# A Nyström attention and MLP kernel: stores issued later, block diagonals by per-head copies, a first batch loaded and cast in finer parts

## Chip, cores, metric

One Trainium2 chip, one core. The metric is the device time of the kernel in microseconds (us), median of several runs. The granted TensorE clock is given where it matters.

## The reference

Eight batches of eight heads (sequence 576, head size 64). Attention is the Nyström form with 32 landmarks, followed by a normalised MLP with a residual:

```python
q_lm, k_lm = q, k averaged over 32 segments of 18 rows
A  = softmax(q k_lm^T / 8);  Bm = softmax(q_lm k_lm^T / 8);  C = softmax(q_lm k^T / 8)
Z  = Bm^T / (norm1(Bm) * norminf(Bm) + 1e-6)
for _ in range(6):
    Z = 2 * Z - Z @ Bm @ Z
x   = A @ Z @ C @ v                      # heads side by side: (8, 576, 512)
out = x + relu(layernorm(x) * g @ w_ch1) @ w_ch2      # 512 -> 2048 -> 512
```

## The kernel before

The MLP of all blocks is one stream of matmuls on TensorE (PE): `fill(n)` issues the next n pieces of it. The attention of later batches is cut into steps, and between two steps the kernel calls `fill`, so PE computes MLP while VectorE (DVE) prepares what attention needs next. GpSimd (POOL) casts the loads of q, k and v to fp16 and sums them. W is the number of units of four heads handled at once: 2, or 4 where two batches go together.

A Newton step of the inverse works on 32x32 blocks, one per head, four heads stacked on the 128 partitions. To do four heads in one matmul, the blocks are spread to a block-diagonal 128x128 matrix, `ebd`. This is done by a product with a 0/1 mask over a broadcast source:

```python
def diagonal(name, src, W, mask):
    t = asm.tile([P, W, 4, LM], FP16, name=name, tag=name, bufs=1)
    dve.tensor_tensor(out=t[:], in0=src[:, :, None, :].broadcast_to([P, W, 4, LM]),
                      in1=mask, op=ALU.mult)
    return t
...
for it in range(6):                                   # in attention2, cut
    lo = 0 if it < 5 else LM
    psn = p1([P, W, LM + D], "psn")
    for w in range(W):
        MM(psn[:, w, lo:], ebd[:, w, :, :].rearrange("p a l -> p (a l)"), st[:, w, lo:])
    stn = asm.tile([P, W, LM + D], FP16, name="st", tag="st")
    dve.scalar_tensor_tensor(out=stn[:, :, lo:], in0=st[:, :, lo:], scalar=2.0,
                             in1=psn[:, :, lo:], op0=ALU.mult, op1=ALU.subtract)
    st = stn
    if it < 5:
        ebd = diagonal("ebd", st[:, :, 0:LM], W, masks(W))
    else:
        bmbd = diagonal("bmbd", bm16, W, maskw[:, 0:W, :, None].broadcast_to([P, W, 4, LM]))
    ...
    yield                                             # the caller fills with MLP here
```

So each step is a chain: psn on PE, st on DVE, ebd on DVE, the next psn on PE. The MLP's output block `ot` is stored (`store(j, ot)`) as soon as it is computed, from SyncE's queue, which also issues the loads and the transposes `xnT` by DMA. In the profiles, psh is the MLP's first product, which reads xnT; nat and natv are the fp16 casts of q, k and of v; asum and s are POOL's sums.

The softmax here doesn't subtract the row's maximum and nothing guards it: scores larger than these inputs give would overflow.

Of the kernel before, what the change touches and what calls it, by code (L numbers as in the profile page):

```python
# [9 lines left out]
FP16 = mybir.dt.float16  # L10
# [3 lines left out]
ALU = mybir.AluOpType  # L14
AX = mybir.AxisListType

P = 128
# [3 lines left out]
def kernel(  # L21
# [55 lines left out]
    def TR(o, i_, idn):  # L77
        keep(nc.tensor.matmul(o, i_, idn, is_transpose=True, tile_position=(0, 0)))


    def load(src, b, u, queue):
        t = stage.tile([P, 2, NJ, D], FP32, name="stg", tag="stg")
        keep(queue.dma_start(
            out=t[:],
            in_=src[b, 4 * u:4 * u + 4].rearrange("(r e) (t j) d -> (e t) r j d", e=2, j=NJ)))
        return t
# [3 lines left out]
    def load_qk(b):  # L90
        for u in range(U):
            raw[b]["q", u] = load(q, b, u, nc.sync)
            raw[b]["k", u] = load(k, b, u, nc.sync)

    def load_v(b):
        for u in range(U):
            raw[b]["v", u] = load(v, b, u, nc.sync)

# [11 lines left out]
    def cast_qk(b, u, nm, engine):  # L110
        t = nat.tile([P, NJ, 2, D], FP16, name="nat", tag="nat")
        engine.tensor_copy(out=t[:].rearrange("p j r d -> p r j d"), in_=raw[b][nm, u][:])
        nat_tiles[b, nm, u] = t
# [51 lines left out]
    maskw = const.tile([P, 4, 4], FP16, name="maskw")  # L165
    mask16 = const.tile([P, 4], FP16, name="mask16")
    nc.gpsimd.tensor_copy(out=mask16[:], in_=mask4[:])
    for w in range(4):
# [21 lines left out]
    pool.tensor_copy(out=natv_buf[0][:, 0:2, :, 0:D], in_=raw[0]["v", 0][:])  # L190
    pool.tensor_copy(out=natv_buf[0][:, 2, :, 0:D], in_=raw[0]["v", 1][:, 0])
    bones = const.tile([P, 4, 32], FP16, name="bones")
    for u in range(U):
# [87 lines left out]

    def diagonal(name, src, W, mask):
        t = asm.tile([P, W, 4, LM], FP16, name=name, tag=name, bufs=1)
        dve.tensor_tensor(out=t[:], in0=src[:, :, None, :].broadcast_to([P, W, 4, LM]),
                          in1=mask, op=ALU.mult)
        return t

    def masks(W):
        return mask16[:, None, :, None].broadcast_to([P, W, 4, LM])


    def attention(bs):
# [13 lines left out]
        for w, (b, u) in enumerate(units):  # L306
            for i, nm in enumerate(("q", "k")):
                n16 = nat_tiles[b, nm, u]
                pst = p2([P, NJ, P], FP16, "pst")

                def sums():
                    for j in range(NJ):
                        MM(pss[:, i, w, :], n16[:, j, :, :].rearrange("p r d -> p (r d)"),
                           pm16[:], start=(j == 0), stop=(j == NJ - 1), skip=True)

                last = (w, i) == (W - 1, 1)
                if last:
                    sums()
                for j in range(NJ):
                    TR(pst[:, j, :], n16[:, j, :, :].rearrange("p r d -> p (r d)"), ident16[:])  # L320
                t = aprep.tile([P, NJ, P], FP16, name="xT", tag="xT" + nm, bufs=5 if nm == "q" else 4)
                if not first and i == 1:
                    dve.tensor_copy(out=t[:], in_=pst[:])
                elif not (first and last):
                    scalar.copy(t[:], pst[:])
                xT[nm, w] = t
                if not last:
                    sums()
                yield
# [10 lines left out]
        if first:  # L340
            dve.tensor_copy(out=t[:], in_=pst[:])
        yield
# [34 lines left out]
        psse_ = p1([P, 4, W * LM], "psse")  # L377
        psse = psse_[:, 0:2, :].rearrange("p a (u l) -> p a u l", u=W)
        for w in range(W):
            for h in range(4):  # L380
                sl = ds(32 * h, 32)
                MM(psse[sl, 1, w, :], bmT[sl, w, :], bmT[sl, w, :], rb=32 * h, cb=32 * h)
        MM(psse[:, 0, :, :], bones[:].rearrange("p a c -> p (a c)"), bm16[:])
        dve.tensor_reduce(out=psse_[:, 2, 0:W], in_=psse[:, 0, :, :], axis=AX.X,
# [9 lines left out]
        if not first:  # L394
            ebd = diagonal("ebd", st[:, :, 0:LM], W, masks(W))

# [3 lines left out]
        for w, (b, u) in enumerate(units):  # L400
            natv = natv_of[b]
            for j in range(NJ):
                for h in range(4):
                    r, e = divmod(h, 2)
                    rows = ds(64 * e, 64)
                    MM(pscv[ds(32 * h, 32), w, :], ect[w][rows, j, ds(32 * r, 32)],
                       natv[rows, 2 * u + r, j, :], rb=64 * e, cb=32 * h,
                       start=(j == 0), stop=(j == NJ - 1), skip=True)
        rcv = asm.tile([P, W], FP32, name="rcv", tag="rcv")
# [7 lines left out]
        for it in range(6):  # L417
# [16 lines left out]
            if not first and it < 5:  # L434
                ebd = diagonal("ebd", st[:, :, 0:LM], W, masks(W))
            if it < W:
# [168 lines left out]
    def attention2(bs, c):  # L605
# [39 lines left out]
        for w in range(W):  # L645
            for h in range(4):
# [11 lines left out]
                                op=ALU.mult)  # L658
        ebd = diagonal("ebd", st[:, :, 0:LM], W, masks(W))


        pscv = ps2.tile([P, 2, 512], FP32, name="pscv", tag="p2")
        for y in range(W // 2):
# [13 lines left out]
            if y + 1 < W // 2:  # L677
                yield
        v_used.update(c.bs)
        pcv = pscv[:, :, 0:(W // 2) * (D + 1)].rearrange("p x (y e) -> p y x e", e=D + 1)  # L680
        rcv = asm.tile([P, W], FP32, name="rcv", tag="rcv")
# [10 lines left out]
        for it in range(6):  # L692
# [9 lines left out]
            if it < 5:  # L702
                ebd = diagonal("ebd", st[:, :, 0:LM], W, masks(W))
            else:
                bmbd = diagonal("bmbd", bm16, W,
                                maskw[:, 0:W, :, None].broadcast_to([P, W, 4, LM]))
            if it < W // 2:
# [168 lines left out]
    def mlp():  # L876
        for g in range(NGRP):
# [44 lines left out]
            for u in range(4):  # L922
# [5 lines left out]
                for m in range(MCH):  # L928
# [4 lines left out]
                    if g == 0 and u >= 2 and m % 8 == 3:  # L933
                        n = len(turned.get(1, ()))
                        if 4 + n in xn_of:
# [4 lines left out]
                                         in1=x_blk.pop(j)[:], op0=ALU.mult, op1=ALU.add)  # L940
                store(j, ot)
                yield True

    stream = mlp()

    def fill(n):
        for _ in range(n):
            if not next(stream, False):
                return


# [6 lines left out]
    warm(50, 128)  # L958
    for _ in range(4):
        run(a0)  # L960
        warm(3, 256)
    run(a0)
    warm(1, 512)
    run(a0)
    scalar.copy(natv_buf[0][:, 3, :, 0:D], raw[0]["v", 1][:, 1])
    warm(1, 512)
# [71 lines left out]
    for i, _ in enumerate(a1):  # L1038
        fill(5 if i < 9 else 7)
        settle()  # L1040
        next_cast()
        if 5 <= i < 11:
            sets[0].next_job()
# [8 lines left out]
    for c, after, count in zip(sets, sets[1:] + [None], counts):  # L1052
        for step, _ in enumerate(attention2(c.bs, c)):
            fill(count[step])
            settle()
            if late and step >= 3:
# [6 lines left out]
        while after and (after.jobs or after.lms):  # L1063
            fill(8)
            next_cast()
            after.next_job()
    for _ in stream:
        pass

# [29 lines left out]
```

## Time and profile before

| | before |
|---|---|
| time, median | 329.6 us |
| span of the profiled run | 327.9 us |
| PE busy, and idle (span less busy) | 314.7, 13.2 us |
| waits of PE for ebd; for xnT | 1.6; 1.4 us |
| ebd: instructions | 30 |

The prediction below shows the lines on busy shares and waits. Here is the one view it names without showing, the instructions on the tile ebd. The columns are duration in ns (minimum, median, maximum), first and last start in us, and the forms.

```profile
L68 DVE TENSOR_TENSOR ebd<-st,mask x30: 424/691/1740, 40.8 to 234.8; 128x256 f16<-128x256 f16 x18, 128x512 f16<-128x512 f16 x12
```

There are two forms (W=2 and W=4). Undisturbed they take 424 and 691 ns.

### The profile page before, as it was taken

How to read it: one execution, taken by the hardware profiler on the slowest of the kernel's cores; microseconds unless marked ns; L12 is line 12 of the kernel's file. 1: busy time of each engine (PE TensorE's matmuls, PEld its weight loads, DVE VectorE, ACT ScalarE, POOL GpSimd, SP SyncE). 2: the span in 40 equal slices, each digit the busy share in tenths (PEclk: the TensorE clock that was granted, in tenths of full speed). 3: DMA queues.
4: the chain of work that ended last, by engine and by line, in shares of the span. 5: the costliest groups of instructions: out<-in, count | busy, mean ns of one | idle time of the engine just before them, and what ended most of it. 6: DMA issues, size and time to landing. Idle time of an engine off the chain costs nothing.

```text
span 327.9 us, 8249 instructions
## 1 busy us (share of the span) xinstructions
PE 314.7 (96%) x3409; PEld 162.3 (50%) x3409; DVE 175.7 (54%) x395; ACT 152.7 (47%) x307; POOL 153.3 (47%) x241
## 2 busy tenths in 40 slices
PE   8889999999999999989999999999999999999995
PEld 8547864553445444435544445454444444444444
DVE  3668769779964797953237668722566120010012
ACT  3546762749960661957204672454046107305600
POOL 3389979999999999999800034100014000000000
PEclk9999999999999999999999999999999999999998
DMA  7999999898797864695022103330242126032023
GB/s 278 394 356 365 366 402 303 297 345 239 241 195 231 234 169 127 156 290 102 4 68 66 34 20 76 82 50 2 64 104 26 32 64 98 0 72 60 0 49 79
DMA packets 36397, 50.34 MB, mean 154 GB/s; under 512 B 17796, under 2 KB 22152, under 8 KB 36360
## 3 DMA queue, kind: packets, MB, share of 16 engines
q1 hardware_dynamic: 36200, 49.69, 52.7%
q8 instruction: 26, 0.43, 0.5%
q10 hardware_dynamic: 160, 0.13, 0.2%
q14 instruction: 11, 0.09, 0.1%
HBM read 36.70 MB, written 9.44 MB: 141 GB/s over the span
## 4 chain that ended last, share of the span: by engine, by line
PE 56%; POOL 22%; DMA 7%; issue 2%; ACT 2%; DVE 1%; SPq 0%; POOLq 0%
PE psh L74 26%; PE pso L74 25%; POOL asum L68 11%; POOL nat L68 6%; POOL natv L68 3%; DMA stg<-in_q_dram 3%; POOL xn L68 2%; DMA w2stg<-in_moe_w_ch_dram 2%; POOL s L68 1%; PE psy L74 1%; PE pscv L74 1%; DMA stg<-in_v_dram 1%; DMA stg<-in_k_dram 1%; DMA xnT<-xn 1%; ACT xn L68 1%
## 5 line engine op out<-in xcount | busy, mean ns | idle before, releaser
L74 PE MATMUL psh<-xnT,w 128*128 128x512 f16 (+1 forms) x640 | 133.7, 358 | 1.4 <-DMA xnT<-xn 1.4
L74 PE MATMUL pso<-w,hT 128*128 128x512 f16 (+1 forms) x592 | 132.9, 374 | 0.0
L68 ACT ACTIVATE hT<-psh 128x512 f16<-128x512 f32 x144 | 84.9, 597 | 97.6 <-PE psh L74 97.4
L74 PEld LDWEIGHTS <-w 128*128 128x128 f16 x640 | 59.5, 98 | 56.7 <-issue 3.1
L74 PEld LDWEIGHTS <-hT 128*128 128x128 f16 x592 | 56.1, 98 | 57.2 <-issue 0.8
L68 DVE SCALAR_TENSOR_TENSOR ot<-pso,rstd,xblk 128x512 f32<-128x512 f32 (+1 forms) x37 | 27.1, 732 | 77.6 <-PE pso L74 77.4
L68 POOL CAST nat<-stg 128x1152 f16<-128x1152 f32 x28 | 32.5, 1167 | 3.4 <-DMA stg<-in_k_dram 1.7
L68 POOL TENSOR_TENSOR asum<-asum 128x256 f32<-128x256 f32 (+2 forms) x54 | 28.4, 527 | 4.2
L68 DVE TENSOR_TENSOR xblk<-psy,rcpd 128x512 f32<-128x512 f32 (+1 forms) x40 | 27.6, 691 | 1.8 <-POOL w L68 0.2
L68 POOL TENSOR_TENSOR asum<-nat 128x576 f32<-128x576 f16 x18 | 23.4, 1299 | 1.5
L68 POOL TENSOR_SCALAR xn<-xblk,mvg 128x512 f16<-128x512 f32 x14 | 9.6, 694 | 30.9 <-ACT junk L68 30.9
L68 DVE SCALAR_TENSOR_TENSOR st<-st,psn 128x192 f16<-128x192 f16 (+3 forms) x36 | 14.2, 395 | 17.6 <-PE psn L74 17.4
L68 POOL CAST natv<-stg 128x1152 f16<-128x1152 f32 (+1 forms) x16 | 17.6, 1119 | 9.6 <-DMA stg<-in_v_dram 9.6
L68 POOL TENSOR_SCALAR negm<-mvg 128x1 f32<-128x1 f32 x14 | 2.7, 191 | 40.5 <-DVE mvg L68 35.9
L68 DVE TENSOR_TENSOR ebd<-st,mask 128x256 f16<-128x256 f16 (+1 forms) x30 | 20.7, 690 | 1.0
L68 DVE STREAM_TRANSPOSE xT<-nat 128x576 uint32<-128x576 uint32 x24 | 18.2, 760 | 2.2 <-POOL nat L68 2.2
L74 PE MATMUL psy<-zcbd,ea 128*128 128x260 f16 (+1 forms) x80 | 15.9, 276 | 1.0 <-DVE xblk L68 0.4
L68 ACT ACTIVATE ea<-psea 128x576 f16<-128x576 f32 x12 | 7.2, 648 | 16.5 <-PE psea L74 16.5
L74 PE MATMUL idle<-zeros 128*128 128x128 f16 (+2 forms) x82 | 13.4, 312 | 1.1 <-DVE eps_ln L172 1.1
L74 PEld LDWEIGHTS <-ea 128*128 128x128 f16 (+1 forms) x80 | 7.1, 100 | 12.2 <-issue 3.5
L68 ACT ACTIVATE junk<-xblk 128x512 f16<-128x512 f32 x14 | 8.8, 625 | 9.4 <-DVE xblk L68 9.2
L68 DVE BATCH_NORM_STATS2 st<-xblk 128x6 f32<-128x512 f32 x18 | 12.4, 688 | 0.5
(115 smaller groups left out, 263.0 us busy)
## 6 DMA issues: line engine op xcount, KB each, us to landing
stg<-in_q_dram SPq DMA_DIRECT2D x16, 576.0 KB, 6.0
stg<-in_k_dram SPq DMA_DIRECT2D x16, 576.0 KB, 5.7
out_dram<-ot SPq DMA_DIRECT2D x70, 128.0 KB, 2.4
stg<-in_v_dram SPq DMA_DIRECT2D x10, 576.0 KB, 6.4
w1stg<-in_moe_w_ch_dram SPq DMA_DIRECT2D x16, 256.0 KB, 6.0
w2stg<-in_moe_w_ch_dram SPq DMA_DIRECT2D x16, 256.0 KB, 5.2
stg<-in_v_dram SPq DMA_DIRECT2D x12, 288.0 KB, 5.5
xnT<-xn SPq DMA_TRANSPOSE x28, 3.3
```

The costliest lines, as they stand in the source:

```text
L68: return lambda *args, **kw: keep(getattr(self.engine, op)(*args, **kw))
L74: keep(nc.tensor.matmul(o, l, r, start=start, stop=stop, tile_position=(rb, cb), skip_group_check=(skip or cb != 0)))
```

## The change

The intent: (a) the first batch's last k comes and is cast in two parts of 5 and 4 of 9, with less filler ahead of psb; (b) the column sums of Bm are formed ahead of Bm's product with itself; (c) the first batch's last v comes in two parts and is cast by ACT and POOL together; (d) four copies, one per head, write the diagonal blocks into a zeroed constant tile; (e) bmbd is made before the Newton steps instead of after them; (f) stores of `ot` are issued one step later, so that SyncE does not wait for `ot` with loads and transposes queued behind. Cut to its core:

```diff
+    ebd = const.tile([P, 4, 4, LM], FP16, name="ebd")
+    nc.gpsimd.memset(ebd[:], 0.0)
...
-    def diagonal(name, src, W, mask):
-        t = asm.tile([P, W, 4, LM], FP16, name=name, tag=name, bufs=1)
-        dve.tensor_tensor(out=t[:], in0=src[:, :, None, :].broadcast_to([P, W, 4, LM]),
-                          in1=mask, op=ALU.mult)
-        return t
+    def diagonal(src, W):
+        for h in range(4):
+            rows = ds(32 * h, 32)
+            dve.tensor_copy(out=ebd[rows, 0:W, h, :], in_=src[rows, :, :])
...
+        for _, j in halves if (b, u, nm) == (0, U - 1, "k") else whole:
+            engine.tensor_copy(out=t[:, j, :, :].rearrange("p j r d -> p r j d"),
+                               in_=raw[b][nm, u][:, :, j, :])
...
+        MM(psse[:, 0, :, :], bones[:].rearrange("p a c -> p (a c)"), bm16[:])
         for w in range(W):
             for h in range(4):
                 MM(psse[sl, 1, w, :], bmT[sl, w, :], bmT[sl, w, :], rb=32 * h, cb=32 * h)
-        MM(psse[:, 0, :, :], bones[:].rearrange("p a c -> p (a c)"), bm16[:])
...
-    scalar.copy(natv_buf[0][:, 3, :, 0:D], raw[0]["v", 1][:, 1])
+    scalar.copy(natv_buf[0][:, 3, 0:5, 0:D], raw[0]["v", 1][:, 1, 0:5])
...
-                store(j, ot)
+                if at_end:
+                    store(j, ot)
+                else:
+                    to_store.append((j, ot))
...
+    def work(n):
+        k = len(to_store)
+        fill(n)
+        settle()
+        for _ in range(k):
+            store(*to_store.pop(0))
```

Cut: the splitting of the loads, the order of the first batch's sums and the split of its transposes, the move of bmbd.

More of the change, by code (lines that the diff above doesn't have):

```diff
@@ L78, in TR, with load @@
         keep(nc.tensor.matmul(o, i_, idn, is_transpose=True, tile_position=(0, 0)))
-    def load(src, b, u, queue):
+    whole = ((slice(0, 2), slice(0, NJ)),)
+    halves = ((slice(0, 2), slice(0, 5)), (slice(0, 2), slice(5, NJ)))
+    pairs = ((slice(0, 1), slice(0, NJ)), (slice(1, 2), slice(0, NJ)))
+    def load(src, b, u, queue, parts=whole):
         t = stage.tile([P, 2, NJ, D], FP32, name="stg", tag="stg")
-        keep(queue.dma_start(
-            out=t[:],
-            in_=src[b, 4 * u:4 * u + 4].rearrange("(r e) (t j) d -> (e t) r j d", e=2, j=NJ)))
+        rows = src[b, 4 * u:4 * u + 4].rearrange("(r e) (t j) d -> r (e t) j d", e=2, j=NJ)
+        for r, j in parts:
+            if parts is halves:
+                for i in range(2):
+                    keep(queue.dma_start(out=t[:, i, j, :], in_=rows[i][:, j, :]))
+            else:
+                keep(queue.dma_start(out=t[:, r, j, :],
+                                     in_=rows[r][:, :, j, :].rearrange("r p j d -> p r j d")))
         return t
@@ L92, in load_qk @@
             raw[b]["q", u] = load(q, b, u, nc.sync)
-            raw[b]["k", u] = load(k, b, u, nc.sync)
+            raw[b]["k", u] = load(k, b, u, nc.sync, halves if (b, u) == (0, U - 1) else whole)
     def load_v(b):
         for u in range(U):
-            raw[b]["v", u] = load(v, b, u, nc.sync)
+            raw[b]["v", u] = load(v, b, u, nc.sync, pairs if (b, u) == (0, U - 1) else whole)
     def load_seg(src, b, u, queue, turned=False):
@@ L111, in cast_qk @@
         t = nat.tile([P, NJ, 2, D], FP16, name="nat", tag="nat")
-        engine.tensor_copy(out=t[:].rearrange("p j r d -> p r j d"), in_=raw[b][nm, u][:])
+        for _, j in halves if (b, u, nm) == (0, U - 1, "k") else whole:
+            engine.tensor_copy(out=t[:, j, :, :].rearrange("p j r d -> p r j d"),
+                               in_=raw[b][nm, u][:, :, j, :])
         nat_tiles[b, nm, u] = t
@@ L165 @@
     maskw = const.tile([P, 4, 4], FP16, name="maskw")
-    mask16 = const.tile([P, 4], FP16, name="mask16")
-    nc.gpsimd.tensor_copy(out=mask16[:], in_=mask4[:])
+    ebd = const.tile([P, 4, 4, LM], FP16, name="ebd")
+    nc.gpsimd.memset(ebd[:], 0.0)
     for w in range(4):
@@ L191 @@
     pool.tensor_copy(out=natv_buf[0][:, 2, :, 0:D], in_=raw[0]["v", 1][:, 0])
+    pool.tensor_copy(out=natv_buf[0][:, 3, 5:NJ, 0:D], in_=raw[0]["v", 1][:, 1, 5:NJ])
     bones = const.tile([P, 4, 32], FP16, name="bones")
@@ L279, in warm @@
             MM(idle[:, 0:cols], zeros[:], zeros[:, None, :].broadcast_to([P, cols // P, P]))
-    def diagonal(name, src, W, mask):
-        t = asm.tile([P, W, 4, LM], FP16, name=name, tag=name, bufs=1)
-        dve.tensor_tensor(out=t[:], in0=src[:, :, None, :].broadcast_to([P, W, 4, LM]),
-                          in1=mask, op=ALU.mult)
-        return t
-    def masks(W):
-        return mask16[:, None, :, None].broadcast_to([P, W, 4, LM])
+    def diagonal(src, W):
+        for h in range(4):
+            rows = ds(32 * h, 32)
+            dve.tensor_copy(out=ebd[rows, 0:W, h, :], in_=src[rows, :, :])
     def attention(bs):
@@ L309, in attention, with sums @@
                 pst = p2([P, NJ, P], FP16, "pst")
-                def sums():
-                    for j in range(NJ):
+                def sums(js=range(NJ)):
+                    for j in js:
                         MM(pss[:, i, w, :], n16[:, j, :, :].rearrange("p r d -> p (r d)"),
@@ L316, in attention @@
                 last = (w, i) == (W - 1, 1)
-                if last:
+                if last and not first:
                     sums()
-                for j in range(NJ):
-                    TR(pst[:, j, :], n16[:, j, :, :].rearrange("p r d -> p (r d)"), ident16[:])
+                for js in (range(0, 5), range(5, NJ)) if first and last else (range(NJ),):
+                    if first and last:
+                        sums(js)
+                    for j in js:
+                        TR(pst[:, j, :], n16[:, j, :, :].rearrange("p r d -> p (r d)"),
+                           ident16[:])
                 t = aprep.tile([P, NJ, P], FP16, name="xT", tag="xT" + nm, bufs=5 if nm == "q" else 4)
@@ L325, in attention @@
                     scalar.copy(t[:], pst[:])
+                else:
+                    scalar.copy(t[:, 0:5, :], pst[:, 0:5, :])
                 xT[nm, w] = t
@@ L340, in attention @@
         if first:
-            dve.tensor_copy(out=t[:], in_=pst[:])
+            dve.tensor_copy(out=t[:, 5:NJ, :], in_=pst[:, 5:NJ, :])
         yield
@@ L394, in attention @@
         if not first:
-            ebd = diagonal("ebd", st[:, :, 0:LM], W, masks(W))
+            diagonal(st[:, :, 0:LM], W)
         v_used.update(bs)
@@ L401, in attention @@
             natv = natv_of[b]
-            for j in range(NJ):
-                for h in range(4):
-                    r, e = divmod(h, 2)
-                    rows = ds(64 * e, 64)
-                    MM(pscv[ds(32 * h, 32), w, :], ect[w][rows, j, ds(32 * r, 32)],
-                       natv[rows, 2 * u + r, j, :], rb=64 * e, cb=32 * h,
-                       start=(j == 0), stop=(j == NJ - 1), skip=True)
+            order = [(j, h) for j in range(NJ) for h in range(4)]
+            if first and w == W - 1:
+                order.sort(key=lambda jh: jh[1] // 2)
+            for j, h in order:
+                r, e = divmod(h, 2)
+                rows = ds(64 * e, 64)
+                MM(pscv[ds(32 * h, 32), w, :], ect[w][rows, j, ds(32 * r, 32)],
+                   natv[rows, 2 * u + r, j, :], rb=64 * e, cb=32 * h,
+                   start=(j == 0), stop=(j == NJ - 1), skip=True)
         rcv = asm.tile([P, W], FP32, name="rcv", tag="rcv")
@@ L434, in attention @@
             if not first and it < 5:
-                ebd = diagonal("ebd", st[:, :, 0:LM], W, masks(W))
+                diagonal(st[:, :, 0:LM], W)
             if it < W:
@@ L658, in attention2 @@
                                 op=ALU.mult)
-        ebd = diagonal("ebd", st[:, :, 0:LM], W, masks(W))
+        diagonal(st[:, :, 0:LM], W)
         pscv = ps2.tile([P, 2, 512], FP32, name="pscv", tag="p2")
@@ L679, in attention2 @@
         v_used.update(c.bs)
+        bmbd = asm.tile([P, W, 4, LM], FP16, name="bmbd", tag="bmbd", bufs=1)
+        dve.tensor_tensor(out=bmbd[:], in0=bm16[:, :, None, :].broadcast_to([P, W, 4, LM]),
+                          in1=maskw[:, 0:W, :, None].broadcast_to([P, W, 4, LM]), op=ALU.mult)
         pcv = pscv[:, :, 0:(W // 2) * (D + 1)].rearrange("p x (y e) -> p y x e", e=D + 1)
@@ L702, in attention2 @@
             if it < 5:
-                ebd = diagonal("ebd", st[:, :, 0:LM], W, masks(W))
-            else:
-                bmbd = diagonal("bmbd", bm16, W,
-                                maskw[:, 0:W, :, None].broadcast_to([P, W, 4, LM]))
+                diagonal(st[:, :, 0:LM], W)
             if it < W // 2:
@@ L940, in mlp @@
                                          in1=x_blk.pop(j)[:], op0=ALU.mult, op1=ALU.add)
-                store(j, ot)
+                if at_end:
+                    store(j, ot)
+                else:
+                    to_store.append((j, ot))
                 yield True
     stream = mlp()
+    to_store, at_end = [], []
     def fill(n):
@@ L958 @@
     warm(50, 128)
-    for _ in range(4):
+    for i in range(4):
         run(a0)
-        warm(3, 256)
+        if i < 3:
+            warm(3, 256)
     run(a0)
-    warm(1, 512)
+    warm(1, 128)
     run(a0)
-    scalar.copy(natv_buf[0][:, 3, :, 0:D], raw[0]["v", 1][:, 1])
+    scalar.copy(natv_buf[0][:, 3, 0:5, 0:D], raw[0]["v", 1][:, 1, 0:5])
     warm(1, 512)
@@ L1038 @@
     for i, _ in enumerate(a1):
-        fill(5 if i < 9 else 7)
-        settle()
+        work(5 if i < 9 else 7)
         next_cast()
@@ L1053 @@
         for step, _ in enumerate(attention2(c.bs, c)):
-            fill(count[step])
-            settle()
+            work(count[step])
             if late and step >= 3:
@@ L1063 @@
         while after and (after.jobs or after.lms):
-            fill(8)
+            work(8)
             next_cast()
             after.next_job()
+    at_end.append(True)
     for _ in stream:
-        pass
+        while to_store:
+            store(*to_store.pop(0))
 _INS = ['q', 'k', 'v', 'moe_g_ln', 'moe_w_ch1', 'moe_w_ch2']
```

## The prediction

> **What bounds the kernel now.** I read the page's busy shares and slices first, then the idle time of TensorE (PE), then the timeline where that idle time lies, then the groups by form for the durations.
>
> ```profile
> PE 314.7 (96%) x3409; PEld 162.3 (50%) x3409; DVE 175.7 (54%) x395; ACT 152.7 (47%) x307; POOL 153.3 (47%) x241
> ...
> PE   8889999999999999989999999999999999999995
> ...
> POOL 3389979999999999999800034100014000000000
> ...
> DMA  7999999898797864695022103330242126032023
> ```
>
> PE is busy for 314.7 of 327.9 us, so 13.2 us are idle; a further 13.4 us of its busy time are the 82 "idle<-zeros" matmuls that only fill waits, 4.9 us of them the opening 50. Everything the change can win must come out of these. The slices show where: PE is below 9 only in the first 30 us, where the DMA row is full too. POOL is full up to slice 19, about 160 us. The busy table by stretches gives the rest:
>
> ```profile
> 50.00:142.00 92.00, 87.44 (x1115) 41.84 (x1114) 74.00 (x153) 53.10 (x122) 86.00 (x114) 1.00 0.80 229
> 142.00:324.00 182.00, 181.92 (x1558) 87.11 (x1556) 68.67 (x151) 72.43 (x138) 32.26 (x54) 1.00 0.28 60
> ```
>
> The columns are the stretch, its length, then busy time of PE, PEld, DVE, ACT, POOL. After 142 us PE has no idle time to give back (0.08 us of 182) until the 4 us tail, which the change leaves alone. Between 50 and 142 us it is idle 92.00 - 87.44 = 4.6 us. The waits of PE by releaser name these:
>
> ```profile
> PE psn L74 <- DVE ebd L68: 1.6, 3, 0.7
> PE psh L74 <- DMA xnT<-xn: 1.4, 1, 1.4
> ```
>
> POOL in that stretch is busy 86.00 of 92 and its remaining 6 us are the short seams between instructions: from 50.4 us on it waits for no transfer, so POOL is a second bound up to 142 us. The one long PE wait, 1.42 us at 141.71, is for the transposed xn, which POOL makes. It is partly SyncE's order; its timeline shows:
>
> ```profile
> 135.75 1.20 SPq L870 DMA_TRANSPOSE xnT<-xn  x1
> 137.04 1.24 SPq L829 DMA_DIRECT2D out_dram<-ot  x2
> 138.38 1.25 SPq L870 DMA_TRANSPOSE xnT<-xn  x1
> ```
>
> Two stores stand between two transposes and take 1.24 us of SyncE's queue just before the transpose that PE waits for.
>
> **What the Trainium skill says.** "VectorE: DVE Perf Modes", section "The perf-mode tier table": a tensor_copy of 16-bit data in SBUF may run at four elements a cycle, a tensor_tensor at two at most. This trace: the 128x256 ebd product takes 0.424 us undisturbed and the 128x512 one 0.691, so 0.267 us for 256 more elements, one a cycle at 0.96 GHz; the broadcast product gets no perf mode here. Same page, "Two Vector instructions with no wait between them": an instruction that starts in another group of 32 partitions than the one before is held until all earlier ones finish. The four copies start at rows 0, 32, 64 and 96, so by that model they don't overlap; nothing in this trace shows it. "SBUF — State Buffer", section "SBUF: two separate sides": VectorE in a two-port mode, or with two SBUF inputs, and GpSimd share a port pair as an exclusive lock for the whole instruction. The trace agrees:
>
> ```profile
> 73.27 3.52 POOL L68 CAST nat<-stg 128x1152 f16<-128x1152 f32 x3
> ...
> 73.76 0.93 DVE L68 TENSOR_TENSOR ebd<-st,mask 128x256 f16<-128x256 f16 x1
> ...
> 26.24 0.56 DVE L68 TENSOR_SCALAR w<-w1stg,g_sb 128x256 f16<-128x256 f32 x1
> ...
> 30.03 0.34 DVE L68 TENSOR_SCALAR w<-w1stg,g_sb 128x256 f16<-128x256 f32 x1
> ```
>
> The product at 73.76 takes 0.93 instead of 0.42: the first POOL cast ends at 73.27 + 1.14 = 74.41, the product 0.28 us later. The one-source w scaling takes 0.34 us when POOL lets it and 0.56 between POOL's instructions. "Perfetto Trace Analysis", section "DMA Optimizations", says that splitting a transfer lets part of the work start sooner where DMA engines are idle. Here they aren't (share 1.05 from 8.2 to 16.4 us), so only the part that lands first gains, not the last byte.
>
> **The change, part by part.**
>
> (a) k in halves. The last k (k1) lands at 9.41, its one cast takes 0.76, sums start at 10.22, take 0.43, and psb starts at 11.64. Cast in 5 and 4 of 9 parts, only the last 0.76 x 4/9 + fixed cost, about 0.40 us, follows the landing (-0.35), 4 instead of 9 sums (-0.2), and the filler before psb shrinks from 1280 to 128 columns (-0.2). psb comes about 0.7 us earlier.
>
> (b) Column sums first. The reduction that starts at 13.57 can start as soon as bm and the transpose are done, about 13.15: another -0.4 on cinv and the left part of st.
>
> (c) v in parts. This is what the first Newton step really waits for:
>
> ```profile
> 13.52 0.67 POOL L68 CAST natv<-stg 128x576 f16<-128x576 f32 x1 [1.44 <-DMA stg<-in_v_dram]
> ...
> 14.24 0.47 PE L74 MATMUL pscv<-natv,ect 64*32 64x65 f16 x36 [0.31 <-POOL natv L68]
> ...
> 14.76 0.17 DVE L68 RECIPROCAL rcv<-pscv 128x2 f32<-128x2 f32 x1 [0.30 <-PE pscv L74]
> ```
>
> v's last byte still lands near 13.5. The 0.67 us cast becomes 5/9 on ACT beside 4/9 on POOL, 0.4 us, and the first pair's product runs ahead. So Newton starts 0.3 to 0.5 us earlier, not the 1.1 us of (a) plus (b): v hides the rest.
>
> (d) Diagonal copies. 30 products go, 120 copies of 32x64 or 32x128 come. Fixed cost of a one-source DVE instruction: 0.343 us less 256/2 cycles (0.133) is 0.21. At four a cycle a copy is 0.02 to 0.03 more, so about 0.2 us alone. If they pipeline as the zcbd casts at 7.2 us do (starts 0.075 apart), four take about 0.4 us: W=2 equal to 0.42, W=4 better than 0.69 by 0.25. If held, about 0.8 us: worse than either. After 165 us POOL is nearly idle and most PE slack between the product and its use is 0.9 to 1.9 us, so there neither matters. In the stretch 40 to 122 us it matters: for nine of the fifteen ebd products that end a Newton step, the timeline has less than 0.2 us from the product's end to the psn matmul that reads it.
>
> (e) bmbd moved off the last step: its 1.16 us at 80.81 sits between st and pszc; worth 0.5 to 1 us of PEld waits ("PEld L74 <- DVE bmbd L68: 0.7" in the waits).
>
> (f) Late stores. Built, the two stores ahead of the second transpose become one, so 0.6 of the 1.42 us wait should go. Bytes are the same.
>
> Sum: of the start, 0.4 us reaches the stream; (d) and (e), where they go well, save 1 to 1.6 us of PE waits. At 141.71 the whole is capped: PE can't be there earlier than xnT, which comes 0.6 us earlier by (f), plus what POOL gains by not being locked out. POOL's excess over its fastest instances is about 3 us in all (for example 18 final sums at 382 against 319 ns and 28 casts at 1167 against 1142); I give 1 us of it to the products. So a gain of 0.6 + 1 us, at most 2.5 us: 327 to 328.5.
>
> **The rivals.**
>
> R1: the copies are locked out one by one. A held copy ends, POOL's next instruction takes the lock, and the next copy waits for all of it. Two one-source DVE instructions in a row under a busy POOL (25.75 to 26.32 and 26.24 to 26.80) did end one per POOL instruction, 0.15 us after each. With POOL instructions of 0.32 to 1.3 us, mean 0.7, four copies then take 0.45 + 3 x 0.7, about 2.5 us, against means of 0.6 to 1.1 us now. With 0.3 us of slack that delays PE by 1 to 1.5 us in each of 15 steps before 142 us: 15 to 20 us, less the 1.4 us that PE waits anyway and the gains above, so 340 to 346. Against it: a copy holds the lock for 0.02 to 0.03 us only, so two or three may slip into POOL's seams (0.08 us and its start-up). That halfway case costs 0 to 6 us: 328 to 334.
>
> R2: all is hidden. Everything up to 142 us is set by POOL and the transfers, the gains turn into a longer wait at 141.7, and the time is 329 to 329.6. The 86 of 92 us of POOL speak for it, the SyncE order against.
>
> R3: more and smaller transfers delay the first loads. k goes from one issue to four, v to two; each issue takes SyncE 0.4 to 0.5 us (0.46 for q now), so v is issued 1.5 us later, at about 4.4, still 6 us ahead of its landing. At most 0.3 us.
>
> **Range and chances.** I give the good course (326.5 to 328.5) 50%, R2 20%, the halfway case 15%, full R1 15%. The middle of that is near 328.3. The low end, 325.5, needs nearly all of the waits up to 142 us back; the high end, 337, leaves most of full R1 outside. Faster by 2% would be under 323, which needs 6.6 us, more than all of PE's waits between 50 and 324 us: 3%. Slower by 2% is over 336.2: most of full R1, 14%.
>
> **What would show it.** (a) to (c): psn starts near 14.9 instead of 15.31, with v still landing near 13.5. (d): the ebd copies' group shows 0.17 to 0.2 us each where POOL idles; in 40 to 122 us, right if the group's maximum stays under 0.5 us, R1 if many take 0.5 to 1.3 us and PE's and PEld's waits for ebd rise over 10 us in sum. (f): the wait of psh for xnT falls under 1 us and the transpose follows the one before it by one store. R2 would show as a longer wait for xnT at an unchanged time. A fall of PE's busy time without the fillers, or of the time before 142 us by over 4 us, would prove me wrong on what bounds it.

## The result, and the profile after

The changed kernel takes 342.4 us (341.5 to 343.2, 6 runs) against 329.6. The ratio is 1.039 (95% interval 1.037 to 1.042): slower. Ratios are the mean time of one kernel's fast runs over that of the other's of the same rounds, so they are not quite the ratio of the medians quoted.

The page of the changed kernel, the lines that answer to those shown of before (busy time, then 40 slices of the span in tenths):

```profile
PE 317.9 (93%) x3406; PEld 162.3 (48%) x3406; DVE 197.1 (58%) x486; ACT 153.4 (45%) x308; POOL 151.1 (44%) x242
...
PE   8889877996699997899999999999999999999995
...
POOL 3489979999428999787960004310003100000000
PEclk9999998999899999999999999999999999999999
```

PE's idle time rose from 13.2 to 341.5 - 317.9 = 23.6 us, by 10.4. Its busy time rose by 3.2, although it does less filling. Together that is the 13.6 us of the longer span. The new holes lie in slices 5 to 17, counted from one, and nothing after 145 us is worse. PE's waits by releaser, with the sum, the count and the longest, all in us:

```profile
PE psn L74 <- DVE ebd L68: 12.3, 10, 3.0
PE psn L74 <- DVE st L68: 2.4, 2, 1.6
```

Before, the first was 1.6 us. The wait for xnT, 1.4 us before, is gone: PE now comes later than the transposes. The waits for ebd and its source rose by 12.8 us in sum (14.7 against 1.9), which covers the 10.4 us of new idle time; other waits shrank. The copies on the tile ebd, in the columns explained above:

```profile
L68 DVE COPY ebd<-st x120: 169/184/1174, 40.6 to 249.3; 32x64 f16<-32x64 f16 x72, 32x128 f16<-32x128 f16 x48
```

One copy takes 169 to 184 ns when nothing disturbs it, and up to 1174 when something does. The timeline of the longest wait shows what. The columns are start, duration, engine, operation and, in brackets, idle time before it; "x4" means four instructions merged in one line:

```profile
84.46 4.41 POOL L68 CAST natv<-stg 128x1152 f16<-128x1152 f32 x4
...
84.49 1.67 PE L74 MATMUL psh<-xnT,w 128*128 128x512 f16 x7
...
85.64 0.34 DVE L68 SCALAR_TENSOR_TENSOR st<-st,psn 128x192 f16<-128x192 f16 x1
86.02 3.08 DVE L68 COPY ebd<-st 32x64 f16<-32x64 f16 x4
...
89.16 0.30 PE L74 MATMUL psn<-st,ebd 128*128 128x96 f16 x2 [2.99 <-DVE ebd L68]
```

Four small copies take 3.08 us while POOL runs four casts of 1.1 us. In the individual records they end 0.04 us or less after the first, second and third POOL cast, with the fourth copy right behind the third. PE has used up its seven MLP matmuls at 86.16 and stands still for 3 us. Where POOL idles, the same four copies look like this:

```profile
185.25 0.79 DVE L68 COPY ebd<-st 32x128 f16<-32x128 f16 x4
...
239.00 0.73 DVE L68 COPY ebd<-st 32x64 f16<-32x64 f16 x4
```

That is 0.73 and 0.79 us, so one copy starts (0.73 - 0.17) / 3 = 0.19 us after the one before: they do not overlap. Twice the elements, 64 more, cost 0.06 / 4 = 0.015 us a copy; the old product needs 0.267 us for 256 more. Per element the copy is thus about four times as fast.

The other 3.2 us are in the PEclk row, which dips in slices 7 and 11 (of 8.5 us each). I cut the trace into stretches of 3.41 us, aligned to where the clock changes. The columns are the stretch, its length, busy time of PE, PEld, DVE, ACT and POOL, the granted clock, DMA share and GB/s:

```profile
48.28:51.69 3.41, 1.69 (x16) 1.04 (x13) 2.97 (x7) 1.14 (x2) 2.77 (x4) 1.00 1.06 363
51.69:55.10 3.41, 1.53 (x11) 0.76 (x12) 2.92 (x9) 0.60 (x1) 3.10 (x6) 1.00 1.02 227
55.10:58.52 3.42, 3.42 (x18) 1.00 (x15) 3.05 (x6) 0.00 (x0) 3.18 (x4) 0.50 1.02 343
...
85.83:89.24 3.41, 0.42 (x4) 0.09 (x3) 3.30 (x6) 1.23 (x3) 3.04 (x3) 1.00 0.71 223
89.24:92.65 3.41, 3.41 (x12) 1.37 (x13) 2.57 (x10) 1.20 (x3) 0.00 (x0) 0.50 0.81 294
```

Twice PE was busy for less than half of such a stretch (1.53 and 0.42 of 3.41 us) and then ran the whole next one at half clock. A stretch at 1.69 us, just under 50%, was not followed by one. By this working each slow stretch does half its work: 1.7 us lost, 3.4 us in two. The trace of before has no half clock between its start and its end.

### The profile page after: what moved, and what is told of

The parts are those of the page before. It is cut to its first block, busy times and chain, and to the rows that moved or that the text cites. A ratio compares the mean times of both kernels' runs of the same rounds, so it can differ in the third digit from the quotient of the medians.

```text
span 341.5 us, 8340 instructions
## 1 busy us (share of the span) xinstructions
PE 317.9 (93%) x3406; PEld 162.3 (48%) x3406; DVE 197.1 (58%) x486; ACT 153.4 (45%) x308; POOL 151.1 (44%) x242
## 4 chain that ended last, share of the span: by engine, by line
PE 70%; DVE 17%; ACT 2%; issue 2%
PE pso L74 33%; PE psh L74 29%; DVE ebd L68 7%; DVE st L68 3%; PE pscv L74 2%; PE psy L74 2%; DVE xT L68 2%; DVE xblk L68 2%; DVE ot L68 1%; ACT xn L68 1%; PE psn L74 1%; DVE lmk L68 1%; PE psec L74 1%; DVE rcv L68 1%; PE psea L74 1%
## 5 line engine op out<-in xcount | busy, mean ns | idle before, releaser
L74 PE MATMUL psh<-xnT,w 128*128 128x512 f16 (+1 forms) x640 | 135.7, 361 | 0.0
L74 PE MATMUL pso<-w,hT 128*128 128x512 f16 (+1 forms) x592 | 134.5, 377 | 0.0
L68 DVE COPY ebd<-st 32x64 f16<-32x64 f16 (+1 forms) x120 | 40.5, 338 | 2.2
L68 POOL TENSOR_TENSOR asum<-asum 128x256 f32<-128x256 f32 (+2 forms) x54 | 27.2, 503 | 4.2
L74 PE MATMUL psn<-st,ebd 128*128 128x96 f16 (+1 forms) x84 | 8.6, 208 | 14.8 <-DVE ebd L68 12.3
L68 POOL CAST natv<-stg 128x1152 f16<-128x1152 f32 (+2 forms) x17 | 17.9, 1075 | 8.8 <-DMA stg<-in_v_dram 8.8
L74 PEld LDWEIGHTS <-ebd 128*128 128x128 f16 x84 | 5.7, 99 | 25.1 <-DVE ebd L68 18.4
L74 PE MATMUL idle<-zeros 128*128 128x128 f16 (+2 forms) x79 | 12.3, 296 | 1.1 <-DVE eps_ln L184 1.1
L68 DVE BATCH_NORM_STATS2 st<-xblk 128x6 f32<-128x512 f32 x18 | 12.4, 688 | 0.5
```

Of the source, the lines that this page charges most:

```text
L68: return lambda *args, **kw: keep(getattr(self.engine, op)(*args, **kw))
L74: keep(nc.tensor.matmul(o, l, r, start=start, stop=stop, tile_position=(rb, cb), skip_group_check=(skip or cb != 0)))
```

## The experiments

**Theory L (lock and hold; both are the rules that the prediction cites).** POOL and a DVE copy in its fast mode exclude each other for the whole instruction, and a copy that starts in another group of 32 rows than the one before is held until that one is done. So after each copy POOL takes the port pair first, and four copies wait for up to four POOL instructions. **Rivals:** (N) number alone, four instructions for one cost 0.8 us wherever they are; (P) another part of the change, the late stores or the split loads, costs part of the 13 us.

| kernel | median, us | ratio to before (95%) | PE idle, us | PE waits for ebd, xnT, us |
|---|---|---|---|---|
| changed | 342.4 | 1.039 (1.037 to 1.042) | 23.6 | 12.3, 0 |
| e1: changed, old product | 329.1 | 1.000 (0.998 to 1.002) | 13.1 | 2.4, 0.7 |
| e2: before, copies only | 341.3 | 1.037 (1.034 to 1.039) | 23.7 | 13.0, 0 |
| e3: blocks from PSUM | 330.1 | 1.002 (0.999 to 1.004) | 14.0 | 4.2 (as st), 0 |
| e4: copies on one row group | 336.6 | 1.024 (1.020 to 1.028) | 18.8 | 8.3, 0 |
| e5: e1, mask in PSUM | 326.0 | 0.989 (0.987 to 0.992) | 10.2 | 0, 0.8 |
| e6: before, start only | 329.7 | 1.001 (0.999 to 1.003) | 12.5 | 1.8, 1.4 |
| e7: before, stores only | 329.3 | 1.000 (0.997 to 1.002) | 12.4 | 1.4, 0.5 |
| e8: e1, copies after 150 us only | 329.3 | 0.999 (0.996 to 1.002) | 14.5 | 2.4, 0.3 |
| e9: e5, all such products | 325.4 | 0.989 (0.987 to 0.991) | 11.0 | 0, 1.3 |
| e10: before, mask in PSUM only | 327.0 | 0.992 (0.990 to 0.995) | 11.3 | 0, 1.2 |

All results are correct except e4's. Its output is wrong, which doesn't matter for the time. PE idle is span less PE busy of the one profiled run, so it does not follow the medians to the tenth.

### e1: the old product back, everything else of the change kept

```diff
-        for h in range(4):
-            rows = ds(32 * h, 32)
-            dve.tensor_copy(out=ebd[rows, 0:W, h, :], in_=src[rows, :, :])
+        dve.tensor_tensor(out=ebd[:, 0:W], in0=src[:, :, None, :].broadcast_to([P, W, 4, LM]),
+                          in1=mask16[:, None, :, None].broadcast_to([P, W, 4, LM]), op=ALU.mult)
```

> The changed kernel with the old broadcast product in place of the four copies; everything else of the change stays (late stores, start, early bmbd). Theory (the copies are locked out by POOL one after another, and nothing else of the change costs): 327 to 329 us, PE's waits for ebd at most 2 us, no stretch of half clock. Rival (something else of the change, the late stores or the split loads, costs part of the 13 us): 332 us or more.

Measured: 329.1 us, ratio 1.000, 0.1 us over the expected range. There is no half clock before the end. The whole loss is the copies', and rival P falls. But the good parts are worth nothing measurable either: waits for ebd even come to 2.4 us, a miss of the expected 2. SyncE's timeline shows that the late stores did what they were meant to:

```profile
135.11 1.21 SPq L890 DMA_TRANSPOSE xnT<-xn  x1
136.37 0.59 SPq L846 DMA_DIRECT2D out_dram<-ot  x1
137.05 1.23 SPq L890 DMA_TRANSPOSE xnT<-xn  x1
```

One store instead of two stands between the transposes, and the last one is issued at 137.05 instead of 138.38. Yet psh starts at 141.31 instead of 141.71, so only 0.4 of these 1.3 us arrive: this transpose took 4.2 us from its issue to its landing, against 3.2 us before.

### e2: the copies alone

```diff
-        ebd = diagonal("ebd", st[:, :, 0:LM], W, masks(W))
+        copies(st[:, :, 0:LM], W)          # the four tensor_copy of the change, at all four places
```

> The kernel before with nothing but the four copies. Theory: the whole loss and a bit more, since bmbd still comes late: 341 to 345 us, copies up to 1.1 us each in the stretch where POOL is full, 0.17 to 0.19 us where it idles. Rival: under 335 us.

Measured: 341.3 us, with one stretch of half clock. The waits of this kernel:

```profile
PEld L74 <- DVE ebd L68: 18.8, 13, 3.9
PE psn L74 <- DVE ebd L68: 13.0, 11, 3.4
```

The copies alone make the loss.

### e3: four instructions in four row groups, none of which needs the second port

```diff
+            if it < 5:
+                for h in range(4):
+                    rows = ds(32 * h, 32)
+                    dve.scalar_tensor_tensor(out=ebd[rows, 0:W, h, :], in0=st[rows, :, 0:LM],
+                                             scalar=2.0, in1=psn[rows, :, 0:LM],
+                                             op0=ALU.mult, op1=ALU.subtract)
             dve.scalar_tensor_tensor(out=stn[:, :, lo:], ...)      # as before
-            if it < 5:
-                diagonal(st[:, :, 0:LM], W)
```

> The changed kernel, but in the Newton steps each block of the diagonal is computed straight from psn (2 st - psn, one operand in PSUM) in four instructions on 32 rows each, so still four and still in four groups of rows, but none that needs the second SBUF port. If the lock is the cause: no block takes over 0.3 us and the time is 328 to 332 us. If holding alone (four instructions one after another, about 0.8 us) is the cause: PE's waits for ebd stay over 8 us and the time is over 337 us.

Measured: 330.1 us. No block of the 100 takes over 0.3 us, as expected. The first block matrix of each set has no psn yet and is still made by four copies, 20 in all; in the same run, under the same POOL, one of them takes 1175 ns. First the tile view (ns), then the timeline of one step with POOL's casts across it:

```profile
L68 DVE SCALAR_TENSOR_TENSOR ebd<-st,psn x100: 166/227/295, 43.0 to 236.1; 32x64 f16<-32x64 f16 x60, 32x128 f16<-32x128 f16 x40
...
L68 DVE COPY ebd<-st x20: 169/194/1175, 40.6 to 216.5; 32x64 f16<-32x64 f16 x12, 32x128 f16<-32x128 f16 x8
```

```profile
73.66 2.23 POOL L68 CAST nat<-stg 128x1152 f16<-128x1152 f32 x2
...
74.33 0.91 DVE L68 SCALAR_TENSOR_TENSOR ebd<-st,psn 32x64 f16<-32x64 f16 x4
```

Four held instructions cost 0.91 us under two POOL casts, more than the product's 0.42 undisturbed, and PE's waits for the st behind them are 4.2 us in sum. POOL, which the product used to delay, is busy for 151.0 us against 153.3; that this makes up for the waits is likely, but no run shows it alone. Number and holding alone (N) therefore do not make the 13 us; they need the lock.

### e4: the copies under the same lock, but not held

```diff
-            rows = ds(32 * h, 32)
+            rows = ds(0, 32)
```

> The changed kernel with all four copies on rows 0 to 31: wrong result on purpose, the same number of copies under the same lock, but none starts in another group of rows than the one before. If holding is what lets POOL in between: copies start 0.08 us apart where POOL idles, two or three slip in after one POOL instruction, and the time falls to 331 to 337 us. If the lock alone decides, holding or not: 341 to 343 us, as the changed kernel.

Measured: 336.6 us, half-way, as expected. The timeline, once where POOL idles and once where it is full:

```profile
79.89 1.14 POOL L68 CAST nat<-stg 128x1152 f16<-128x1152 f32 x1
80.20 2.22 DVE L68 COPY ebd<-st 32x64 f16<-32x64 f16 x4
81.12 1.27 POOL L68 TENSOR_TENSOR asum<-nat 128x576 f32<-128x576 f16 x1
...
235.34 0.43 DVE L68 COPY ebd<-st 32x64 f16<-32x64 f16 x4
```

Where POOL idles, four take 0.43 us instead of 0.73: starts (0.43 - 0.17) / 3 = 0.09 us apart. Under the full POOL, individual records show copies one to three ending at 81.07, 81.15 and 81.24, right behind the cast that ends at 81.04; only the fourth waits for the next POOL instruction and ends at 82.42. In the changed kernel's step shown above, three POOL casts came between. Without the lock the time is 330.1, without holding 336.6, with both 342.4: no loss is seen without the lock, and holding makes about half of it.

### e8: the copies only where POOL is nearly idle

```diff
-        diagonal(st[:, :, 0:LM], W)
+        (by_head if bs[0] >= 5 else diagonal)(st[:, :, 0:LM], W)     # by_head: the four copies
```

> e1 with the four copies in the last two sets of batches alone (after 165 us, where POOL is nearly idle), the product in the sets before. If it is the lock against a busy POOL: the copies there take 0.17 to 0.19 us each, PE's slack hides the 0.74 us, and the time is that of e1, 328.8 to 329.6. If four instructions for one cost by themselves: 331 us or more.

Measured: 329.3 us, the time of e1, with 48 of the 120 copies in place:

```profile
L68 DVE COPY ebd<-st x48: 169/180/515, 156.9 to 235.8; 32x128 f16<-32x128 f16 x24, 32x64 f16<-32x64 f16 x24
```

Their median is 0.18 us and one at 157 us, where POOL still works, takes 0.5. The same instructions cost nothing measurable there.

### e6 and e7: the start alone, the stores alone

e6 is the kernel before with (a), (b) and (c); e7 with (f). Their diffs are those parts of the change (e6, like e1, keeps ebd as a constant tile).

```diff
-        fill(5 if i < 9 else 7)            # e7, at each place that fills
-        settle()
+        work(5 if i < 9 else 7)            # fill, settle, then the stores left over from the last time
```

> The kernel before with only the start of the change (k and v in parts, column sums first, shorter fillers). By the prediction psn starts 0.3 to 0.5 us earlier than 15.31 and the time is 329.0 to 329.4 (before 329.4), the gain ending as a longer wait for xnT near 141 us. Rival R3: later loads make it 329.5 to 330.5.

> The kernel before with only the late stores. By the prediction the wait of psh for xnT falls from 1.42 us to 0.8 us or less and the time by as much: 328.6 to 328.9. Rival: the time that is won there is waited for elsewhere, 329.4.

Measured: 329.7 and 329.3 us; neither can be told from before (ratios 1.001 and 1.000, intervals of 0.2 to 0.25% each way). In e6's profile the first psn starts at 15.34 us, in before's at 15.31, in e1's at 15.19, in the changed kernel's at 15.15. Over all twelve profiles it starts at 15.07 to 15.34 us with the new start (eight kernels, mean 15.16) and at 15.18 to 15.72 without (four, mean 15.41). The gain there is thus about 0.25 us, within the spread of single profiles. In e6 the second q, which the change does not touch, is cast at 8.11 us, in before's profile at 7.89, in e7's at 8.46. Loads vary by more than the start could win. In e7 the wait for xnT fell to 0.5 us, as expected, but the time by only 0.3 us in the medians, less than the 0.7 expected and inside the noise. The rival fits: e7's trace has a new idle time of PE, 1.1 us before the psh at 110.8 us, for which the profile names no cause (0.55 us at the same place in e1, none in before). e6's 329.7 lies in the range given to R3, but its interval holds no change as well.

### e5, e10, e9: taking the lock away from the product

If L holds, the spread of the old product (424 to 1740 ns) is the same lock: it has two operands in SBUF. "SBUF — State Buffer", section "Who interferes with whom", states that a VectorE instruction with at most one SBUF input, outside the two-port modes, does not contend with GpSimd. So the 0/1 mask goes to PSUM, four fp32 numbers per partition in the end of a bank that had room:

```diff
+    bank1 = ps1.tile([P, 512], FP32, name="bank1", tag="p1")     # the bank of psb, psse, psn, ...
+    maskp = bank1[:, 508:512]
+    dve.tensor_copy(out=maskp, in_=mask4[:])
...
-                          in1=mask16[:, None, :, None].broadcast_to([P, W, 4, LM]),
+                          in1=maskp[:, None, :, None].broadcast_to([P, W, 4, LM]),
```

(psse is packed from 4 W x 32 to 2 W x 32 + 2 W columns to leave the room, and the mask is now fp32 where it was fp16. No run changes these two without the place of the mask.)

> e1 (everything of the change but the copies) with one thing more: the mask of the diagonal product lies in PSUM, so the product has one operand in SBUF and should need no second port. If the lock is the cause of the product's spread too, no ebd product takes over 0.8 us (before: up to 1.74), PE's wait for ebd falls from 2.4 us to under 1 us, and the time is 327.3 to 328.5 us. If the spread has another cause (operands of the product late, say), the maximum stays over 1.2 us and the time at 329.

Measured: 326.0 us, ratio 0.989, 1.3 us better than the forecast range. The tile view (ns), then the timeline of a product under two POOL casts:

```profile
L68 DVE TENSOR_TENSOR ebd<-st,bank x30: 420/422/687, 40.6 to 230.6; 128x256 f16<-128x256 f16 x18, 128x512 f16<-128x512 f16 x12
```

```profile
72.37 2.24 POOL L68 CAST nat<-stg 128x1152 f16<-128x1152 f32 x2
...
73.70 0.42 DVE L68 TENSOR_TENSOR ebd<-st,bank 128x256 f16<-128x256 f16 x1
```

Every product takes its undisturbed time. PE has no wait for ebd left, POOL's casts to nat go from a mean of 1167 to 1147 ns, and xnT is ready at 137.6 instead of 141.7 us. PE had only 2 us of waits for ebd and st before; the rest of the gain goes with POOL coming earlier, and with it the bound at xnT. That reading is from the traces; no run separates the two.

e10 is that edit, the mask in PSUM, in the kernel before, with nothing of the change:

> The kernel before with one thing alone: the mask of the ebd product in PSUM. If the gain of e5 (326.0) is the lock's alone, this one reaches 326.0 to 327.0 and xnT is ready near 138 us in place of 141.7; if e5 needed the rest of the change (late stores, early bmbd), it stays at 328 or more.

Measured: 327.0 us for the kernel before with the mask alone, ratio 0.992, as expected; xnT is ready at 139.0 us, a little later than forecast. So most of the gain comes with the mask's move alone. e5 is 0.3% better by the ratios (0.989 against 0.992), the intervals touch, and the two were not run in the same rounds; whether the rest of the change adds a little once the lock is gone stays open.

e9 is e5 with the reciprocals and bmbd's mask in PSUM too:

```diff
-        dve.reciprocal(out=rcv_, in_=pcv[:, :, :, D])
-        dve.tensor_tensor(out=rcv[:], in0=rcv[:], in1=cinv[:], op=ALU.mult)
+        rcvp = bank1[:, 484:484 + W]
+        dve.reciprocal(out=rcvp.rearrange("p (y x) -> p y x", x=2), in_=pcv[:, :, :, D])
+        dve.tensor_tensor(out=rcv[:], in0=rcvp, in1=cinv[:], op=ALU.mult)
...
-                          in1=maskw[:, 0:W, :, None].broadcast_to([P, W, 4, LM]), op=ALU.mult)
+                          in1=maskwp[:, 0:W, :, None].broadcast_to([P, W, 4, LM]), op=ALU.mult)
```

> e5 with the other products of two SBUF operands freed in the same way: bmbd's mask in PSUM too, and the reciprocal that is multiplied by cinv. bmbd took up to 1.1 us and rcv up to 1.0 us under a full POOL; with the lock as cause bmbd takes at most 0.75 us and rcv under 0.25 us. They are off PE's path mostly, so 325.0 to 326.3 us; if they cost PE nothing, the same as e5.

Measured: 325.4 us, ratio 0.989. The tile views of e5, then of e9:

```profile
L68 DVE TENSOR_TENSOR bmbd<-bm,maskw x4: 381/550/1106, 68.8 to 211.1; 128x256 f16<-128x256 f16 x2, 128x512 f16<-128x512 f16 x2
...
L68 DVE TENSOR_TENSOR rcv<-rcv,cinv x4: 160/162/1042, 69.3 to 216.0; 128x2 f32<-128x2 f32 x2, 128x4 f32<-128x4 f32 x2
```

```profile
L68 DVE TENSOR_TENSOR bmbd<-bm,bank x4: 381/544/677, 69.0 to 211.5; 128x256 f16<-128x256 f16 x2, 128x512 f16<-128x512 f16 x2
...
L68 DVE TENSOR_TENSOR rcv<-bank,cinv x4: 159/160/161, 69.7 to 216.4; 128x2 f32<-128x2 f32 x2, 128x4 f32<-128x4 f32 x2
```

Of the four products of 2 or 4 numbers per partition, one took 1.04 us with both operands in SBUF; with one in PSUM none takes over 0.161. The time cannot be told from e5's, which fits products that are not on PE's path. e5 and e9 are 1.1% faster than the kernel before, and by the ratios to before about 5% faster than the changed one.

## Why the prediction was wrong

- **The bound** was read rightly. The loss lies before 145 us, where POOL is full, and PE's idle time after it stayed nil in both kernels. (One reading of the slices is off: PE is below 9 not only in the first 30 us but also in the slice from 139 to 148 us, which holds the wait for xnT.)
- **(d), one copy alone**: 0.2 us predicted, 0.17 to 0.18 measured; held rather than pipelined, 0.8 us for four predicted, 0.73 to 0.79 measured. Right, where POOL idles.
- **The failed step** is (d) under a full POOL. The forecast of 327 to 328.5 put four copies there at 0.4 us, or 0.8 if held, and counted 1 to 1.6 us of saved PE waits from (d) and (e). In the fifteen steps before 142 us the four took 1.7 us on average, and PE's waits for ebd and st rose by 12.8 us. R1 was the course that came, with 340 to 346 against 342.4, and so were its signs: 22 of the 72 copies before 142 us took over 0.5 us, and PEld's waits for ebd rose from 4.4 to 18.4 us, PE's from 1.6 to 12.3. What led to the choice of the good course is this argument: "a copy holds the lock for 0.02 to 0.03 us only, so two or three may slip into POOL's seams". The reasons for the opposite stood beside it: two one-source DVE instructions that ended one per POOL instruction, and a model under which copies are held. Taken together they leave little seam: in the step at 86 us POOL's next cast began about 0.1 us before each of the next two copies did. e4 shows the seam as it is: in its step at 80 us two more copies slip in at 0.09 us apart, when they are not held. R1 needed the greater weight, not 15%.
- **R1's own terms** were off and made up for each other, so that 342.4 fell into its range is in part luck. Four copies in the 15 steps were put at 2.5 us; the records give a mean of 1.7 (0.7 to 3.1), against 0.76 for the product. 15 x 0.93 = 14 us by this working, and PE's waits for ebd and st rose by 12.8. What R1 left out is the half clock after the long waits, 3.4 us in two stretches.
- **(a) to (c)**: psn starts at 15.15 instead of 15.31, 0.16 us earlier where 0.3 to 0.5 were predicted; in e6 it is not earlier at all, and over all profiles about 0.25 us. v hides the rest, as said, but the last v was not cast earlier either: its last part began at 13.60 us, against 13.52. R3's delay may be in this, but loads that the change leaves alone vary more (7.53 to 8.54 us for the second q in the twelve profiles), so that stays open.
- **(f)**: the order of issue came out as predicted, with the wait for xnT at 0.7 us in e1 and 0.5 in e7, under 1 us as predicted; in time it is not measurable.
- **(e)**: predicted 0.5 to 1 us. No run tried it alone. PEld's waits for bmbd, 0.7 us in before, are gone in e1, but within e1's ratio of 1.000 that did not show.
- **R2** gives the time of the rest of the change: e1, e6 and e7 are all the same as before. Its sign, a longer wait for xnT, did not come: that wait fell in e1 and e7 and stayed at 1.4 us in e6. That POOL's chain up to xnT decides, as R2 said, is borne out from the other side: in e5 and e10, where POOL was freed, xnT and the end both came earlier.
- **The low end** held that waits before 142 us cap the gain at 2.5 us. e5 gained 3.5. The 3 us of POOL's excess were estimated rightly, but the 1 us of it that I gave to the products was too small: with the product alone freed, POOL is busy 3.1 us less in e10 than in before (2.2 us less in e5).

## What to carry to other kernels

An instruction is not cheap because it is short: if it needs a port that a full engine holds back to back, each held instruction can cost one turn of that engine. Here one long instruction (329.1 us) beat four short ones (342.4), and one that doesn't need the port beat both (326.0). Look at the spread between minimum and maximum of one form in the tile view before counting instructions; a product that takes 424 ns and sometimes 1740 is probably queuing behind something, and the timeline shows behind which engine. A small constant operand moved to PSUM took a two-operand VectorE instruction out of that queue here, and it sped up the other engine too. All this is from one kernel.

## What the Trainium skill lacked or had wrong

- "VectorE: DVE Perf Modes", section "Two Vector instructions with no wait between them": the hold agrees with these runs, but the section gives no cost. Copies of 32x64 start 0.19 us apart held and 0.09 us apart when not held (changed kernel and e4).
- "SBUF — State Buffer", section "Who interferes with whom": the lock agrees. It lacks what happens with several short VectorE instructions in a row: held copies wait for one GpSimd instruction after another (3.08 us for four), unheld ones can pass three at a time (e4, step at 80 us).
- The same section states the way out that e5 uses, but no page turns it into advice: a broadcast mask in PSUM instead of SBUF took the product from anything between 424 and 1740 ns to a steady 0.42 us (W=2) or 0.69 us (W=4), and the kernel from 329.5 to 326.0 us in e5 and to 327.0 alone in e10. No page lists a PSUM operand as a means against contention.
- "TensorE: Matmul & The Clock Gate", section "Part 1: The HAM clock gate": says that the clock halves after at least one idle window of about 3.4 us. It does not say how much work such a window may hold. Here windows of 3.41 us with PE busy 45% (1.53 us) and 41% (1.41 us, e4) were followed by a window at half clock, and two at just under 50% (1.69 us, one here and one in e4) were not.
